# Sharing the top-k product and mask among VectorE, GpSimd and ScalarE

## The chip, the cores and the metric

The kernel runs on one core of one Trainium2 chip. The metric is the device time of one execution in microseconds, taken as the median of several runs. The engines are TensorE (PE, with its weight loads shown apart as PEld), VectorE (DVE), ScalarE (ACT), GpSimd (POOL) and SyncE (SP, which issues the transfers). Each engine works through its own instructions in the order in which the program gives them and waits where an operand of another engine is not there yet.

## The reference

Attention keeps, for every query row, only the 32 largest of its 576 scores. Its output is then routed through a mixture of eight experts, each of which takes at most 80 tokens.

```python
# attention: batch 8, heads 8, sequence 576, head dimension 64
scores = scale * np.matmul(q, k.transpose(0, 1, 3, 2))
kth = np.partition(scores, -32, axis=-1)[..., -32:-31]
scores = np.where(scores >= kth, scores, -1e9)
scores = scores - np.max(scores, axis=-1, keepdims=True)
attn = np.exp(scores)
attn = attn / (np.sum(attn, axis=-1, keepdims=True) + 1e-9)
x = np.matmul(attn, v)            # then reshaped to 4608 tokens x 512
# experts: for each e the 80 tokens with the largest gate among those that chose e
h = np.maximum(x[tok_idx] @ w1[e], 0.0)
out[tok_idx] = gate_w[tok_idx, None] * (h @ w2[e])
```

## The kernel before

The attention is cut into 288 units. A unit is 128 query rows of one head (or the last 64 rows of two heads together), so it is a tile of 128 rows by 576 scores. A pair of heads `n` has 9 units: four row blocks with two heads each (`h` is 0 and then 1), and one unit with the rests of both heads (`h` is 2). There are 32 pairs of heads. Below, the position of a unit in its nine is 0 to 8; positions 1, 3, 5 and 7 are those with `h == 1`, and position 8 is the one with `h == 2`.

A unit passes through these stages.

```python
def front(self, n, t):      # TensorE: scores of one row block; ScalarE: into SBUF, times 2^-48
    ...
    nc.scalar.activation(s[...], ps[...], Act.Copy, scale=TINY)

def parts(self, i):         # VectorE: the 8 largest of each of 6 sixths of the row -> 48 candidates
    for j in range(NG):
        nc.vector.max(out=cand[:, j, :], in_=s[:, j * S // NG : (j + 1) * S // NG])
        yield

def search(self, i):        # VectorE: the 24th largest; then ranks 25 to 32 from the row itself
    for r in range(G0 // 8):                                   # G0 = 24
        nc.vector.max(out=dst, in_=cand)
        if r == G0 // 8 - 1:
            sign = self.rows.tile([P, S], BF16, name="sign", tag="sign")
            nc.scalar.activation(sign, s, Act.Sign, bias=w9[:, 7:8], scale=-1.0, accum_out=cnt)
        yield
        if r < G0 // 8 - 1:
            nc.vector.match_replace(out=cand, in_to_replace=dst, in_values=cand, imm_value=LOW)
            yield
    y = self.rows.tile([P, S], F32, name="y", tag="y", bufs=1)        # one buffer
    nc.vector.tensor_tensor(out=y, in0=s, in1=sign, op=Alu.mult)      # the product
    yield
    nc.vector.max(out=w9[:, 8:], in_=y)                               # max of the product
    yield
    nc.vector.scalar_tensor_tensor(out=pick, in0=past, scalar=cnt, in1=w9[:, 7:],
                                   accum_out=self.thr[:, i : i + 1], ...)   # the threshold
    yield

def below(self, i):         # GpSimd: 1 where the score is below the threshold
    engine = nc.vector if i == NU - 1 else nc.gpsimd
    engine.tensor_scalar(self.mask[i], self.s[i], self.thr[:, i : i + 1], None, op0=Alu.is_lt)

def turn_w(self, n, t):     # TensorE: transposed scores, minus the transposed mask; ScalarE: Exp
    ...                     # transposes of s into PSUM (tiles ab and cc)
    nc.tensor.matmul(dst[h][c], lhsT=mk[:, keys[c]], rhs=minus, ...)  # minus = -1 on the diagonal
    nc.scalar.activation(wT[...], cc[...], Act.Exp, scale=scale / TINY)
    nc.scalar.activation(wT[...], ab[...], Act.Exp, scale=scale / TINY)
```

As the scores carry a factor of 2^-48 and the Exp takes it back, a mask of 1 becomes minus 2^48 in the exponent, and the weight becomes 0. `back` multiplies the weights by v (with a column of ones for the sums), `over` takes the reciprocal of the sums on VectorE, `divide` applies it on ScalarE, and `norm` stores the rows and forms the gates.

The stages of several units are interleaved by hand. Step `i` hands out VectorE's work by a string of letters:

```python
back = dict(a=0, b=1, c=1, d=1, e=1, y=2, g=3, h=4, m=4)
for c in "GhmbGcGdGeGGgayz":
    # G: one of the six maxima of unit i's sixths    a: the first max over its candidates
    # b, d: match_replace of unit i-1   c, e: max of unit i-1; with e goes its Sign on ScalarE
    # y: the product of unit i-2   g: the max of the product of unit i-3
    # h: the threshold of unit i-4   m: its mask   z: the reciprocals
    ...
if whole(i - 4): self.turn_w(*units[i - 4][:2])     # where h is 1 or 2
...                                                  # divide
if busy: self.front(*units[i + 4][:2])               # where h of unit i+4 is 0 or 2
if whole(i - 5): self.back(*units[i - 5][:2])
...                                                  # turn of the next q and k, norm
```

Of the kernel before, what the change touches and what calls it, by code (L numbers as in the profile page):

```python
# [10 lines left out]
BF16 = mybir.dt.bfloat16  # L11
# [3 lines left out]
Act = mybir.ActivationFunctionType  # L15
Alu = mybir.AluOpType
# [3 lines left out]
EPS = 1e-9  # L20
LOW = -3.0e38
FAR = 1e-30
TINY = 2.0 ** -48


@with_exitstack
def kernel(
# [11 lines left out]
    nc = tc.nc  # L39
# [8 lines left out]
    scale = 1.0 / math.sqrt(D)  # L48
    P = 128
# [15 lines left out]
    const = ctx.enter_context(tc.tile_pool(name="const", bufs=1))  # L65
# [5 lines left out]
    ident = const.tile([P, P], F32, name="ident")  # L71
# [26 lines left out]
    minus = const.tile([P, P], BF16, name="minus")  # L98
    nc.scalar.mul(minus, ident, -1.0)

    w1_t, w2_t = {}, {}

    def load_w(e, pool, parts=1):
# [19 lines left out]
    class Attention:  # L123


        def __init__(self, stack, lean):
            self.lean = lean
            pool = lambda name, bufs, **kw: stack.enter_context(tc.tile_pool(name=name, bufs=bufs, **kw))
            self.nat, self.qkp, self.rows = pool("nat", 1), pool("qkp", 2), pool("rows", 2)
            self.small, vpool = pool("small", 4), pool("vpool", 1)  # L130
            self.ps_s, self.ps_w, self.ps_c = (pool(n, k, space=PSUM) for n, k in (("ps_s", 1), ("ps_w", 1), ("ps_c", 2)))
            self.qk, self.turned, self.lg = {}, {}, {}
            self.s, self.top, self.cnt, self.y, self.mask, self.w, self.xn = ({} for _ in range(7))
            self.thr, self.z = thr_all, z_all


            self.vb = []
            for j in range(1 if lean else 3):
                t = vpool.tile([P, NK, 2, D + 1], F32, name=f"vb{j}")
                nc.gpsimd.memset(t[:, :, :, D : D + 1], 1.0)  # L140
                nc.gpsimd.memset(t[: P - TL, NF, :, :], 0.0)
                self.vb.append(t)

            self.xT = vpool.tile([P, NK * P], F32, name="xT")
            nc.gpsimd.memset(self.xT[:, S:], 0.0)
# [40 lines left out]
        def front(self, n, t):  # L186
# [12 lines left out]
            for h in range(g):  # L199
                self.s[i + h] = s[:, h * S : (h + 1) * S]  # L200
            nc.scalar.activation(s[:, : g * S].rearrange("p (j c) -> p j c", c=HS), ps[:, : 2 * g, :HS], Act.Copy, scale=TINY)  # L201

# [9 lines left out]
        def search(self, i):  # L212

            s, cand = self.s[i], self.top[i]
            top = self.top[i] = self.small.tile([P, G0 // 8 - 1, 8], F32, name="top", tag="top")
            w9 = self.small.tile([P, 16], F32, name="w9", tag="w9")
            for r in range(G0 // 8):
                dst = top[:, r, :] if r < G0 // 8 - 1 else w9[:, :8]
# [4 lines that stand above are left out]
                    cnt = self.small.tile([P, 1], F32, name="cnt", tag="cnt")  # L223
# [3 lines that stand above are left out]
                    nc.vector.match_replace(out=cand, in_to_replace=dst, in_values=cand, imm_value=LOW)  # L227
                    yield
            y = self.rows.tile([P, S], F32, name="y", tag="y", bufs=1)
            nc.vector.tensor_tensor(out=y, in0=s, in1=sign, op=Alu.mult)  # L230
            yield
            nc.vector.max(out=w9[:, 8:], in_=y)  # L232
            yield
            pick = self.small.tile([P, TOP_K - G0 + 1], F32, name="pick", tag="pick")
            nc.vector.scalar_tensor_tensor(out=pick, in0=past, scalar=cnt, in1=w9[:, 7:], accum_out=self.thr[:, i : i + 1],  # L235
                                           op0=Alu.is_equal, op1=Alu.mult)
            yield

        def below(self, i):

            self.top.pop(i)
            self.mask[i] = self.rows.tile([P, S], BF16, name="mask", tag="mask", bufs=3)

            engine = nc.vector if i == NU - 1 else nc.gpsimd
            engine.tensor_scalar(self.mask[i], self.s[i], self.thr[:, i : i + 1], None, op0=Alu.is_lt)  # L245
# [19 lines left out]
        def turn_w(self, n, t):  # L265

            i = n * UPP + 2 * t
            g = 2 if t < NF else 1
            ab = self.ps_w.tile([P, 2, NF, P], F32, name="ab", tag="ab")
            cc = self.ps_c.tile([P, 512], F32, name="cc", tag="cc")  # L270
            keys = [slice(c * P, c * P + P) for c in range(NF)] + [slice(S - P, S)]
            dst = [[ab[:, h, c, :] for c in range(NF)] + [cc[:, h * P : (h + 1) * P]] for h in range(g)]

            for h in range(g):
                sc = self.s.pop(i + h)
                for c in range(NK):
                    nc.tensor.matmul(dst[h][c], lhsT=sc[:, keys[c]], rhs=ident, start=c == 0 or (c == NF and h == 0), stop=False,  # L277
                                     is_transpose=True, skip_group_check=True)
            for h in range(g):
                mk = self.mask.pop(i + h)  # L280
                for c in (NF, *range(NF)):
                    nc.tensor.matmul(dst[h][c], lhsT=mk[:, keys[c]], rhs=minus, start=False, stop=True, skip_group_check=True)  # L282
            wT = self.rows.tile([P, 2 * NK, P], F32, name="wT", tag="wT")
            nc.scalar.activation(wT[:, 2 * NF : 2 * NF + g, :].rearrange("p h r -> p (h r)"), cc[:, : g * P], Act.Exp,  # L284
                                 scale=scale / TINY)
            nc.scalar.activation(wT[:, : g * NF, :], ab.rearrange("p h c r -> p (h c) r")[:, : g * NF, :], Act.Exp, scale=scale / TINY)  # L286
            self.w[n, t] = wT, cc
# [95 lines left out]
        def run(self, slow):  # L383

            units = []
            for n in range(NP):
                for t in range(NF):
                    units += [(n, t, 0), (n, t, 1)]
                units.append((n, NF, 2))
            first, second = {}, {}  # L390
            later = []
            due = []
# [7 lines left out]
            def step(i, last):  # L400
                if 0 <= i < NU:
                    n, t, h = units[i]
# [6 lines left out]
                    first[i] = self.parts(i)  # L409

                back = dict(a=0, b=1, c=1, d=1, e=1, y=2, g=3, h=4, m=4)
                for c in "GhmbGcGdGeGGgayz":
                    if c == "G":
                        if 0 <= i < NU:
                            next(first[i])
                    elif c == "a":
                        if 0 <= i < NU:
                            next(first[i], None)
                            second[i] = self.search(i)
                            next(second[i])  # L420
                    elif c == "z":
                        for u in drawn:
                            self.over(*u)
                    elif c == "m":
                        if 0 <= i - back[c] < NU:
                            self.below(i - back[c])
                    elif i - back[c] in second:
                        next(second[i - back[c]])
# [27 lines left out]
            with tc.manual_schedule():  # L456
# [4 lines left out]
                i = -4  # L461
# [233 lines left out]
    def finish(wpool, full):  # L695
# [85 lines left out]
        def judge():  # L781


            least = sl.tile([P, 4], F32, name="least")
            nc.vector.tensor_reduce(least[:, 0:1], thr_all, axis=AX, op=Alu.min)
            nc.vector.tensor_reduce(least[:, 1:2], z_all.rearrange("p n c h -> p (n c h)"), axis=AX, op=Alu.min)
            nc.vector.tensor_scalar(least[:, 1:2], least[:, 1:2], -FAR, None, op0=Alu.add)
            for i, most in enumerate((TOP - 1, cap)):
                nc.vector.tensor_scalar(least[:, 2 + i : 3 + i], count[:, i : i + 1], -1.0, most + 0.5, op0=Alu.mult, op1=Alu.add)
            one = sl.tile([P, 1], F32, name="one")  # L790
            nc.vector.tensor_reduce(one, least, axis=AX, op=Alu.min)
            ps = ps_x.tile([P, 512], F32, name="jp", tag="x")
            nc.tensor.transpose(ps[:1, :P], one, ident)
            low = sl.tile([1, 1], F32, name="low")
            nc.vector.tensor_reduce(low, ps[:1, :P], axis=AX, op=Alu.min)
            nc.vector.tensor_scalar(bad, low, 0.0, None, op0=Alu.is_le)
# [78 lines left out]
```

## Time and profile before

The time is 1110.77 us, the median of 3 runs from 1108.79 to 1112.42 us. The profiled run has a span of 1108.5 us. Attention is the part of it up to about 957 us, where the last mask starts; then come routing and the experts.

| engine | busy, us | share of the span |
|---|---|---|
| VectorE | 978.4 | 88% |
| TensorE | 936.7 | 85% |
| TensorE weight loads | 745.3 | 67% |
| ScalarE | 711.1 | 64% |
| GpSimd | 513.4 | 46% |

The shares are averages over the whole span, and they hide that the part after attention leaves VectorE, ScalarE and GpSimd nearly idle. To see what bounds attention, the span has to be read in stretches, and then the chain of work that ended last.

### The profile page before, as it was taken

The page shows a single profiled execution, that of the slowest core. Times are in us where ns is not written, and L with a number is a line of the kernel's source. Part 1 is how long each engine was busy: PE and PEld are TensorE (multiplying, and loading weights), DVE is VectorE, ACT ScalarE, POOL GpSimd, SP SyncE. Part 2 cuts the span into 40 slices and gives each one's busy share as a digit, 9 for nine tenths or more (in the row PEclk, how much of TensorE's full clock was granted, in tenths as well). Part 3 has the DMA queues.
Part 4 walks back from the last instruction along what each step waited for, and adds up shares of the span by engine and source line. Part 5 has one row for each costly group of instructions (what it writes and reads, how often), then busy time and mean ns, then how long its engine had stood idle before and what let it go on. Part 6 is the DMA issues. An engine that isn't in the chain of part 4 may idle for free.

```text
span 1108.5 us, 36039 instructions
## 1 busy us (share of the span) xinstructions
PE 936.7 (85%) x13381; PEld 745.3 (67%) x13381; DVE 978.4 (88%) x5214; ACT 711.1 (64%) x1542; POOL 513.4 (46%) x331
## 2 busy tenths in 40 slices
PE   5889888888888988888888888887988888769896
PEld 3767666666676766667666666666766666658786
DVE  4999999999999999999999999999999999771110
ACT  3777777777777777777677777776777777500110
POOL 1555555555455555555455555554455555401110
PEclk9999999999999999999999999999999999888999
DMA  4244443333333222233322211111111100043911
GB/s 97 62 120 120 112 111 79 83 83 83 83 83 72 70 67 71 73 83 82 81 72 74 82 45 44 45 44 45 44 43 43 32 18 12 13 163 119 361 53 29
DMA packets 167896, 85.79 MB, mean 77 GB/s; under 512 B 117792, under 2 KB 154656, under 8 KB 167712
## 3 DMA queue, kind: packets, MB, share of 16 engines
q1 hardware_dynamic: 166688, 80.78, 26.7%
q0 software_dynamic: 1024, 2.62, 0.8%
q8 instruction: 107, 1.75, 0.7%
q14 instruction: 77, 0.63, 0.2%
HBM read 63.19 MB, written 20.19 MB: 75 GB/s over the span
## 4 chain that ended last, share of the span: by engine, by line
DVE 84%; PE 12%; ACT 2%; another core or an unknown queue 1%; issue 0%; DMA 0%; POOL 0%; SPq 0%; POOLq 0%; DVEq 0%; ACTq 0%
DVE cand L208 25%; DVE y L230 19%; DVE w L232 17%; DVE cand L227 9%; DVE top L219 6%; DVE pick L235 3%; PE yp L765 3%; DVE w L219 3%; PE warm L621 2%; DVE z_all L312 1%; PE sp L196 1%; PE cc L300 1%; PE acc L690 0%; PE ab L277 0%
## 5 line engine op out<-in xcount | busy, mean ns | idle before, releaser
L245 POOL TENSOR_SCALAR mask<-s,thr_all 128x576 bf16<-128x576 f32 x287 | 494.0, 1721 | 465.8 <-DVE cand L227 455.9
L208 DVE MAX8 cand<-s 128x8 f32<-128x96 f32 x1728 | 399.2, 245 | 9.4 <-ACT s L201 9.4
L224 ACT ACTIVATE sign<-s,w 128x576 bf16<-128x576 f32 x288 | 225.9, 784 | 101.6 <-DVE w L219 98.3
L300 PEld LDWEIGHTS cc<-vb,wT 128*64 128x64 f32 x5760 | 213.5, 146 | 65.6 <-ACT wT L286 41.1
L300 PE MATMUL cc<-vb,wT 128*64 128x65 f32 x5760 | 236.0, 233 | 2.8 <-ACT wT L286 2.8
L196 PE MATMUL sp<-kT,qT 64*128 64x288 f32 (+1 forms) x1280 | 211.2, 451 | 14.7 <-ACT part L344 6.1
L230 DVE TENSOR_TENSOR y<-s,sign 128x576 f32<-128x576 f32 x288 | 218.5, 759 | 3.9 <-ACT sign L224 3.6
L232 DVE MAX8 w<-y 128x8 f32<-128x576 f32 x288 | 213.6, 742 | 0.0
L282 PEld LDWEIGHTS <-mask 128*128 128x128 bf16 x1440 | 92.6, 98 | 145.1 <-POOL mask L245 143.0
L277 PE MATMUL ab<-ident,s 128*128 128x128 f32 x1152 | 176.9, 282 | 1.8 <-ACT wT L286 1.7
L201 ACT ACTIVATE s<-sp 128x1152 f32<-128x1152 f32 (+1 forms) x160 | 166.9, 1043 | 16.0 <-PE sp L196 15.9
L282 PE MATMUL cc<-minus,mask 128*128 128x128 bf16 x288 | 64.8, 225 | 119.2 <-POOL mask L245 118.3
L286 ACT ACTIVATE wT<-ab 128x1024 f32<-128x1024 f32 (+1 forms) x160 | 150.5, 941 | 0.1
L196 PEld LDWEIGHTS sp<-kT,qT 64*128 64x128 f32 (+1 forms) x1280 | 109.0, 184 | 54.9 <-ACT part L344 8.0
L277 PEld LDWEIGHTS ab<-ident,s 128*128 128x128 f32 x1152 | 128.5, 142 | 25.3 <-ACT wT L286 15.9
L219 DVE MAX8 top<-cand 128x8 f32<-128x48 f32 x576 | 110.4, 192 | 0.1
L227 DVE MATCH_REPLACE8 cand<-top,cand 128x48 f32<-128x48 f32 x576 | 110.2, 191 | 0.0
L282 PE MATMUL ab<-minus,mask 128*128 128x128 bf16 x1152 | 110.1, 220 | 0.0
L321 ACT ACTIVATE xn<-cc,z_all 128x64 f32<-128x64 f32 (+1 forms) x320 | 82.8, 316 | 31.4 <-DVE z_all L312 31.4
L277 PE MATMUL cc<-ident,s 128*128 128x128 f32 x288 | 79.2, 275 | 0.1
L284 ACT ACTIVATE wT<-cc 128x256 f32<-128x256 f32 (+1 forms) x160 | 58.7, 367 | 27.2 <-PE cc L282 25.9
L235 DVE SCALAR_TENSOR_TENSOR pick<-past,cnt,w 128x9 f32<-128x9 f32 x288 | 60.8, 211 | 0.0
(186 smaller groups left out, 812.2 us busy)
## 6 DMA issues: line engine op xcount, KB each, us to landing
w<-in_moe_w_dram SPq DMA_DIRECT2D x32, 512.0 KB, 4.4
w<-in_moe_w_dram SPq DMA_DIRECT2D x8, 2048.0 KB, 13.1
out_dram<-zero SPq DMA_DIRECT2D x9, 1024.0 KB, 5.9
qn<-in_q_dram SPq DMA_DIRECT2D x64, 128.0 KB, 2.5
kn<-in_k_dram SPq DMA_DIRECT2D x64, 128.0 KB, 2.5
vb<-in_v_dram SPq DMA_DIRECT2D x64, 128.0 KB, 2.5
xd<-xn SPq DMA_DIRECT2D x32, 256.0 KB, 4.3
qn<-in_q_dram SPq DMA_DIRECT2D x32, 32.0 KB, 2.4
```

The costliest lines, as they stand in the source:

```text
L196: nc.tensor.matmul(o, lhsT=qT[d, t * P : t * P + m], rhs=kT[d, j * HS : (j + 1) * HS], start=True, stop=True)
L201: nc.scalar.activation(s[:, : g * S].rearrange("p (j c) -> p j c", c=HS), ps[:, : 2 * g, :HS], Act.Copy, scale=TINY)
L208: nc.vector.max(out=cand[:, j, :], in_=s[:, j * S // NG : (j + 1) * S // NG])
L219: nc.vector.max(out=dst, in_=cand)
L224: nc.scalar.activation(sign, s, Act.Sign, bias=w9[:, 7:8], scale=-1.0, accum_out=cnt)
L227: nc.vector.match_replace(out=cand, in_to_replace=dst, in_values=cand, imm_value=LOW)
L230: nc.vector.tensor_tensor(out=y, in0=s, in1=sign, op=Alu.mult)
L232: nc.vector.max(out=w9[:, 8:], in_=y)
L245: engine.tensor_scalar(self.mask[i], self.s[i], self.thr[:, i : i + 1], None, op0=Alu.is_lt)
L277: nc.tensor.matmul(dst[h][c], lhsT=sc[:, keys[c]], rhs=ident, start=c == 0 or (c == NF and h == 0), stop=False, is_transpose=True, skip_gr ...
L282: nc.tensor.matmul(dst[h][c], lhsT=mk[:, keys[c]], rhs=minus, start=False, stop=True, skip_group_check=True)
L300: nc.tensor.matmul(cc[r : r + TL, o], lhsT=wT[:, j * NF + c if c < NF else 2 * NF + j, r0 : r0 + TL], rhs=vb[:, c, h, :], start=(c == 0), ...
```

## The change

For the 128 units of positions 1, 3, 5 and 7 ("odd" in the code) the product `y` goes from VectorE to GpSimd, and the mask goes from GpSimd to ScalarE. There the mask is no comparison but Relu(threshold - score): positive below the threshold, 0 elsewhere. It can be as small as one rounding step of a score, so it is multiplied by a diagonal of minus 2^100 in place of minus 1. Products of all units still share one buffer `y`, so a product cannot start until the max of the product before it has been taken, and the order of the letters is changed with it: in a step whose product is GpSimd's, the product comes directly behind the max `g` that frees the buffer, and in the others it stays near the end. The purpose is to relieve VectorE by engines that have time left.

```diff
+    huge = const.tile([P, P], BF16, name="huge")
+    nc.scalar.mul(huge, ident, -HUGE)                 # HUGE = 2.0 ** 100
 ...
             y = self.rows.tile([P, S], F32, name="y", tag="y", bufs=1)
-            nc.vector.tensor_tensor(out=y, in0=s, in1=sign, op=Alu.mult)
+            engine = nc.gpsimd if i in self.odd else nc.vector
+            engine.tensor_tensor(out=y, in0=s, in1=sign, op=Alu.mult)
 ...
             self.mask[i] = self.rows.tile([P, S], BF16, name="mask", tag="mask", bufs=3)
+            if i in self.odd:
+                nc.scalar.activation(self.mask[i], self.s[i], Act.Relu, bias=self.thr[:, i : i + 1], scale=-1.0)
+                return
 ...
-                    nc.tensor.matmul(dst[h][c], lhsT=mk[:, keys[c]], rhs=minus, ...)
+                    nc.tensor.matmul(dst[h][c], lhsT=mk[:, keys[c]], rhs=huge if i + h in self.odd else minus, ...)
 ...
+            self.odd = {i for i, unit in enumerate(units) if unit[2] == 1}
 ...
-                for c in "GhmbGcGdGeGGgayz":
+                for c in "hmgyGbGcGdGGGeaz" if i - 2 in self.odd else "hmgGbGcGdGeGGyaz":
```

One more VectorE instruction on a single column, near the end, adapts a test on the smallest threshold to the new mask (`least` in the diff's last part); it runs once.

More of the change, by code (lines that the diff above doesn't have):

```diff
@@ L22 @@
 FAR = 1e-30
+HUGE = 2.0 ** 100
 TINY = 2.0 ** -48
@@ L134, in __init__ @@
             self.thr, self.z = thr_all, z_all
+            self.odd = set()
             self.vb = []
@@ L281, in turn_w @@
                 for c in (NF, *range(NF)):
-                    nc.tensor.matmul(dst[h][c], lhsT=mk[:, keys[c]], rhs=minus, start=False, stop=True, skip_group_check=True)
+                    nc.tensor.matmul(dst[h][c], lhsT=mk[:, keys[c]], rhs=huge if i + h in self.odd else minus, start=False, stop=True, skip_group_check=True)
             wT = self.rows.tile([P, 2 * NK, P], F32, name="wT", tag="wT")
@@ L785, in judge @@
             nc.vector.tensor_reduce(least[:, 0:1], thr_all, axis=AX, op=Alu.min)
+            nc.vector.tensor_scalar(least[:, 0:1], least[:, 0:1], -1.0 / HUGE, None, op0=Alu.add)
             nc.vector.tensor_reduce(least[:, 1:2], z_all.rearrange("p n c h -> p (n c h)"), axis=AX, op=Alu.min)
```

## The prediction

> **What bounds the kernel now.** I read the busy shares in 40 slices first, because totals mix attention with what comes after it:
>
> ```profile
> PE   5889888888888988888888888887988888769896
> DVE  4999999999999999999999999999999999771110
> ACT  3777777777777777777677777776777777500110
> POOL 1555555555455555555455555554455555401110
> ```
>
> VectorE is full from the second slice to about the 34th, that is, through all of attention; ScalarE is at seven tenths and GpSimd at five. Asked for the stretch of 25 to 957 us, the view by stretches gives:
>
> ```profile
> 25.00:957.00 932.00, 798.84 (x10817) 624.59 (x10813) 931.13 (x5043) 683.23 (x1477) 489.15 (x285) 0.97 0.26 68
> ```
>
> The columns are length, PE, PEld, DVE, ACT and POOL busy, granted clock, DMA share, GB/s. VectorE works 931.13 of 932.00 us. The only wait that the list of waits has for it there is 0.3 us, for a sign. So attention lasts as long as VectorE's instructions do. The chain that ended last says the same:
>
> ```profile
> DVE 84%; PE 12%; ACT 2%; another core or an unknown queue 1%; issue 0%; DMA 0%; POOL 0%; SPq 0%; POOLq 0%; DVEq 0%; ACTq 0%
> DVE cand L208 25%; DVE y L230 19%; DVE w L232 17%; DVE cand L227 9%; DVE top L219 6%; DVE pick L235 3%; PE yp L765 3%; DVE w L219 3%; PE warm L621 2%; DVE z_all L312 1%; PE sp L196 1%; PE cc L300 1%; PE acc L690 0%; PE ab L277 0%
> ```
>
> The product is 19% of it: 0.19 x 1108.5 / 288 = 0.73 us for each unit. The groups show what it and its neighbours cost:
>
> ```profile
> L245 POOL TENSOR_SCALAR mask<-s,thr_all 128x576 bf16<-128x576 f32 x287 | 494.0, 1721 | 465.8 <-DVE cand L227 455.9
> L224 ACT ACTIVATE sign<-s,w 128x576 bf16<-128x576 f32 x288 | 225.9, 784 | 101.6 <-DVE w L219 98.3
> L230 DVE TENSOR_TENSOR y<-s,sign 128x576 f32<-128x576 f32 x288 | 218.5, 759 | 3.9 <-ACT sign L224 3.6
> L232 DVE MAX8 w<-y 128x8 f32<-128x576 f32 x288 | 213.6, 742 | 0.0
> ```
>
> For the length of a step I took the timeline of VectorE and of GpSimd around 506 us:
>
> ```profile
> 505.19 0.76 DVE L230 TENSOR_TENSOR y<-s,sign 128x576 f32<-128x576 f32 x1
> 505.87 0.25 DVE L208 MAX8 cand<-s 128x8 f32<-128x96 f32 x1
> 506.04 0.21 DVE L235 SCALAR_TENSOR_TENSOR pick<-past,cnt,w 128x9 f32<-128x9 f32 x1
> 506.18 0.08 DVE L235 DVE_READ_ACCUMULATOR pick<-past,cnt,w 128x1 f32 x1
> ...
> 507.56 0.74 DVE L232 MAX8 w<-y 128x8 f32<-128x576 f32 x1
> 508.23 0.19 DVE L219 MAX8 top<-cand 128x8 f32<-128x48 f32 x1
> 508.41 0.76 DVE L230 TENSOR_TENSOR y<-s,sign 128x576 f32<-128x576 f32 x1
> ```
>
> ```profile
> 506.45 1.72 POOL L245 TENSOR_SCALAR mask<-s,thr_all 128x576 bf16<-128x576 f32 x1 [1.49 <-DVE cand L227]
> ```
>
> Durations overlap, so starts count: the product holds VectorE from 505.19 to 505.87, 0.68 us, and there are 0.18 us from the `top` to the product, where a `top` elsewhere is followed after 0.11. The rest of the step, 505.87 to 508.41, is 2.54 us. The mask starts 0.19 us after the threshold (506.18 + 0.08 to 506.45) and ends at 508.17, before the next product at 508.41.
>
> **What the Trainium skill says.** (1) "SBUF — State Buffer", section "Who interferes with whom": a VectorE instruction with two SBUF inputs contends with a GpSimd instruction that reads SBUF; one with a single SBUF input and outside the two-port modes doesn't. In the trace the 31 products between 449 and 550 us last 757 to 760 ns, and those I followed lie clear of the masks; the maxima, with one input, last 245 ns beside a mask or not. So the trace agrees on the second half and doesn't show the first. (2) "GPSIMD Engine Reference", section 3.1: a `tensor_tensor` of 2048 fp32 takes 4497 ns on GpSimd. In proportion, 576 elements are an estimate of 1.26 us; with some fixed cost and a bf16 input I take 1.35. No run here shows it, and the mask's 1721 ns for one input warns that it may be more. (3) "ScalarE: Activation LUTs", section "What ACT_TABLE_LOAD costs": with a pointer bias 280 + 0.833 N ns, and neighbours overlap by 93 ns. For 576 that is 760; the trace's Sign has 784, which I use for the Relu. Section "Table sets: the hidden batching unit" has Relu in every set; the trace agrees, with one table load in all although Sign, Exp and Relu are used.
>
> **The change part by part.**
>
> *Products leave VectorE.* 128 units x 0.73 us (0.68 for the instruction, about 0.06 for the gap ahead of it) = 93 us.
>
> *GpSimd's product in an ordinary odd step.* It may start when `g` has freed the buffer and must be done when `g` comes again. A step without its product is 2.54 + 0.09 for the reciprocal - 0.06 for the gap = 2.57 us; `g` takes 0.67 of it (507.56 to 508.23), so 1.90 lie between. From these go 0.07 (the max's 0.74 outlasts its slot), 0.19 for GpSimd to start, as with the mask, and an estimated 0.06 for VectorE to see the end: a window of 1.58 us. A product of 1.35 fits with 0.23 to spare. Cost 0.
>
> *Where mask and product fall in one step.* If unit i-2 is at position 1, unit i-4 is at position 8, whose mask is still GpSimd's and ahead of the product. The mask starts 0.41 us into the step (0.22 for the threshold, 0.19) and ends at 2.13; the product ends at 3.48, and VectorE sees it at 3.54. It wants it at 2.57 + 0.21 for the next threshold = 2.78. That is a stall of 0.76 us, once in a pair of heads: 31 x 0.76 = 24 us back.
>
> *Relu on ScalarE.* 128 x (0.784 - 0.093) = 88 us more, off VectorE's path. ScalarE goes from 683 us to 771 in a stage of some 875: 88% on average. But three steps of nine (positions 5, 7 and 0 of unit i) have nearly all of it: Relu 0.7, Sign 0.9 with its accumulator, two Exp 1.25, two `xn` 0.5, scores copy 1.1, together 4.45 us in a step of 2.57. The Sign of the next step stands behind that and ends 7.0 us after the start of the pair of steps, where GpSimd wants it at 2.57 + 3.28 + 1.1 = 7.0. So there is no reserve, and the copies `xT`, `qT` and `kT` (0.64 each) can push it later. I put down 0.2 us for two such steps in a pair of heads: 32 x 2 x 0.2 = 13 us back.
>
> *VectorE's remaining products.* In even steps the product comes some 2.4 us into the step and the mask ends at 2.13, so they should not meet: 0.
>
> *TensorE.* Instructions and shapes are the same; the Relu mask may be there 1.0 us earlier (0.78 in place of 1.72). 799 us of 875 is 91%: close, with 118 us that it now waits for masks as the reserve.
>
> *Once:* the new diagonal and the extra instruction, under 1 us together.
>
> Sum: 1110.8 - 93 + 24 + 13 = 1055 us, 5.0% less.
>
> **The rivals.** (a) *GpSimd's product becomes the wait.* If it takes 2.2 us in place of 1.35, it is 0.62 over its window in 96 ordinary steps and 1.6 late in 31: 60 + 50 = 110 us, more than the 93 gained, and the time is about 1125. For it speaks the mask, 2.99 ns an element where the page's product has 2.2; against it, the changed order gives the product its window right behind `g`, which nobody would need for a slow one. At 1.6 us the time would be near 1075. (b) *ScalarE becomes the bound.* Its load is uneven, and a late Sign delays GpSimd's product, this the max, and this VectorE. At 0.6 us in all 96 heavy pairings it would cost 58 us: about 1100. Against it: 12% are free on average, and the light steps (position 3 and 4) let it catch up. (c) *TensorE becomes the bound.* Its 91% would have to grow by a tenth, or its clock to sink; the records show 0.97 over attention. Then the stage would stop near 880 to 900 us: 1060 to 1080. (d) *All is hidden and GpSimd is quick.* With a product of 1.1 us the one collision shrinks to 0.5 us and the Sign has reserve: about 1033.
>
> **Range and chances.** Most uncertain is GpSimd's duration, then the late Signs; both act as stalls of tenths of a microsecond in some 130 places, so 10 to 40 us. Downwards there are only the 37 us of stalls that I put in, most of which stay. I take 1030 to 1092. Faster by over 2% means under 1088.6: 0.83. Within 2%: 0.11. Slower by over 2% needs a product beyond 2.2 us: 0.06.
>
> **What the profile of the changed kernel would show.** If right: 128 GpSimd products of about 1.35 us; 160 products left on VectorE at 759 ns; VectorE still busy over nine tenths in attention, with waits of its max for GpSimd's `y` of 20 to 45 us, mostly 0.7 to 0.8 us long, one in nine units; 128 Relus of 0.78 us and ScalarE near 770 us in attention; VectorE's products rarely longer than 760 ns. If GpSimd's products are over 1.6 us, the max waits in all odd units, and (a) holds. If GpSimd's product itself waits for the Sign more than some tenths of a microsecond, (b) holds. If the candidates' maxima wait for the scores' copy, or the reciprocals for TensorE, (c) holds. Longer products or thresholds on VectorE would mean that the engines contend where I assumed they don't meet. It would be wrong in whole if attention still ended near 957 us.

## The result and the profile after

| | median, us | runs, us | ratio to before, 95% interval |
|---|---|---|---|
| before | 1111.38 | 1108.79 to 1112.42 | |
| changed | 1028.34 | 1026.38 to 1029.23 | 0.9254 [0.9231, 0.9276] |

The change takes off 83 us. The prediction had 56, and the result lies 1.7 us below its range. The busy slices of the changed kernel's page:

```profile
PE   5889999999889999989899999998999998598896
DVE  3999999999999999999999999999999999551000
ACT  3888899888888898888898888898888988401110
POOL 1444555554454545554454544555454554211101
```

VectorE still fills attention. ScalarE has gone from seven tenths to eight or nine. The stretch of attention, 25 to 880 us (columns: length, PE, PEld, DVE, ACT, POOL busy, granted clock, DMA share, GB/s):

```profile
25.00:880.00 855.00, 767.11 (x10859) 610.74 (x10857) 853.36 (x4929) 760.15 (x1612) 435.80 (x287) 1.00 0.28 74
```

VectorE works 853.36 of 855.00 us, ScalarE 760.15 (89%; predicted 88%) and TensorE 767.11 (90%; predicted 91%). The groups of the operations concerned:

```profile
L254 POOL TENSOR_SCALAR mask<-s,thr_all 128x576 bf16<-128x576 f32 x159 | 273.7, 1721 | 199.6 <-PE ab L291 130.6
L236 POOL TENSOR_TENSOR y<-s,sign 128x576 f32<-128x576 f32 x128 | 164.0, 1281 | 240.3 <-ACT sign L229 104.2
L238 DVE MAX8 w<-y 128x8 f32<-128x576 f32 x288 | 217.4, 755 | 2.2 <-POOL y L236 2.0
L236 DVE TENSOR_TENSOR y<-s,sign 128x576 f32<-128x576 f32 x160 | 118.2, 739 | 3.1 <-ACT sign L229 2.6
L250 ACT ACTIVATE mask<-s,thr_all 128x576 bf16<-128x576 f32 x128 | 99.5, 777 | 0.4 <-DVE pick L241 0.4
L241 DVE SCALAR_TENSOR_TENSOR pick<-past,cnt,w 128x9 f32<-128x9 f32 x288 | 83.6, 290 | 0.0
```

GpSimd's product takes 1281 ns (I took 1350), the Relu 777 (784). Three things are not as foretold: VectorE's max shows hardly any wait for GpSimd's product, 2.0 us in place of 20 to 45; its own products are shorter, 739 ns in place of 759; and the threshold `pick`, 211 ns before, has a mean of 290. The timelines of VectorE and GpSimd at one long threshold (start, duration, instruction) show the last:

```profile
509.69 0.21 DVE L224 MAX8 top<-cand 128x8 f32<-128x48 f32 x1
509.81 1.00 DVE L241 SCALAR_TENSOR_TENSOR pick<-past,cnt,w 128x9 f32<-128x9 f32 x1
510.75 0.08 DVE L241 DVE_READ_ACCUMULATOR pick<-past,cnt,w 128x1 f32 x1
510.82 0.76 DVE L238 MAX8 w<-y 128x8 f32<-128x576 f32 x1
```

```profile
507.75 1.72 POOL L254 TENSOR_SCALAR mask<-s,thr_all 128x576 bf16<-128x576 f32 x1 [4.60 <-DVE pick L241]
509.51 1.28 POOL L236 TENSOR_TENSOR y<-s,sign 128x576 f32<-128x576 f32 x1
```

This is the foretold collision: a mask of position 8 and behind it the product of position 1. But VectorE's stall isn't shown as idle time of the max. It is inside the threshold, which starts at 509.81 and ends at 510.81, just after GpSimd's product (509.51 + 1.28 = 510.79). Taken by position, only the thresholds of position 0 are long, 907 ns on average; two others in the whole run exceed 300 ns. The page puts 130.6 us of GpSimd's idle time before its masks down to TensorE, as if a mask had waited for its buffer; but every mask of position 8 starts 0.19 us after the end of its own threshold, as in the kernel before, so the collision isn't a lack of mask buffers.

### The profile page after: what moved, and what is told of

Read it like the earlier page. It is cut to its first block, busy times and chain, and to the rows that moved or that the text cites. A ratio compares the mean times of both kernels' runs of the same rounds, so it can differ in the third digit from the quotient of the medians.

```text
span 1027.5 us, 35579 instructions
## 1 busy us (share of the span) xinstructions
PE 902.3 (88%) x13381; PEld 728.9 (71%) x13381; DVE 896.0 (87%) x5087; ACT 786.2 (77%) x1671; POOL 456.1 (44%) x331
## 4 chain that ended last, share of the span: by engine, by line
DVE 54%; PE 30%; ACT 11%; issue 2%; another core or an unknown queue 1%; DMA 0%; SPq 0%; POOL 0%; POOLq 0%; ACTq 0%; DVEq 0%
DVE cand L213 17%; DVE w L238 12%; PE cc L309 7%; DVE cand L232 6%; DVE y L236 6%; DVE pick L241 4%; DVE top L224 4%; PE yp L776 3%; PE sp L201 3%; PE ab L286 3%; ACT wT L295 3%; PE sp L178 2%; ACT sign L229 2%; PE warm L632 2%; DVE w L224 2%
## 5 line engine op out<-in xcount | busy, mean ns | idle before, releaser
L213 DVE MAX8 cand<-s 128x8 f32<-128x96 f32 x1728 | 387.0, 244 | 9.5 <-ACT s L206 9.5
L254 POOL TENSOR_SCALAR mask<-s,thr_all 128x576 bf16<-128x576 f32 x159 | 273.7, 1721 | 199.6 <-PE ab L291 130.6
L309 PEld LDWEIGHTS cc<-vb,wT 128*64 128x64 f32 x5760 | 201.2, 139 | 111.5 <-ACT wT L295 94.6
L236 POOL TENSOR_TENSOR y<-s,sign 128x576 f32<-128x576 f32 x128 | 164.0, 1281 | 240.3 <-ACT sign L229 104.2
L309 PE MATMUL cc<-vb,wT 128*64 128x65 f32 x5760 | 223.4, 225 | 52.1 <-ACT wT L295 52.1
L201 PE MATMUL sp<-kT,qT 64*128 64x288 f32 (+1 forms) x1280 | 202.0, 435 | 14.7 <-ACT part L353 6.1
L236 DVE TENSOR_TENSOR y<-s,sign 128x576 f32<-128x576 f32 x160 | 118.2, 739 | 3.1 <-ACT sign L229 2.6
L224 DVE MAX8 top<-cand 128x8 f32<-128x48 f32 x576 | 114.4, 199 | 0.1
L250 ACT ACTIVATE mask<-s,thr_all 128x576 bf16<-128x576 f32 x128 | 99.5, 777 | 0.4 <-DVE pick L241 0.4
L241 DVE SCALAR_TENSOR_TENSOR pick<-past,cnt,w 128x9 f32<-128x9 f32 x288 | 83.6, 290 | 0.0
```

Source lines behind the costliest of these rows:

```text
L201: nc.tensor.matmul(o, lhsT=qT[d, t * P : t * P + m], rhs=kT[d, j * HS : (j + 1) * HS], start=True, stop=True)
L236: engine.tensor_tensor(out=y, in0=s, in1=sign, op=Alu.mult)
L309: nc.tensor.matmul(cc[r : r + TL, o], lhsT=wT[:, j * NF + c if c < NF else 2 * NF + j, r0 : r0 + TL], rhs=vb[:, c, h, :], start=(c == 0), ...
```

## The experiments

The kernels are compared with the kernel before on the same chip; where I speak of sums, they are intervals from the start of a VectorE instruction to the start of the next, added up by kind over the trace. "Nine units" is the mean time for a pair of heads, the time from the first threshold to the last times 9/287: 29.42 us before, 26.90 changed.

**1. The order of the letters alone.** The kernel before, with VectorE keeping every product:

```diff
-                    for c in "GhmbGcGdGeGGgayz":
+                    for c in "hmgGbGcGdGeGGyaz":
```

> The kernel before with only the letters reordered, in all steps as the changed kernel has them where VectorE keeps the product; no work moves to another engine. Theory (part of the gain is the order, not the engines): the product now comes long after the max that frees its buffer, so the gap of 0.065 us goes and the products shrink from 759 to about 740 ns: 288 x (0.065 + 0.02) = 24 us less, about 1087 us, ratio 0.978. Rival (the order is only there to make the engines fit): 1111 us, ratio 1.00.

Measured: 1084.12 us, ratio 0.9765 [0.9745, 0.9786]; nine units take 28.55 us, and the products 738 ns, as the theory had it. So 26.6 us, nearly a third of what the whole change brings, are to be had without moving any work.

**2. Two buffers for the product.** The kernel before in its own order. Two product buffers beside three mask buffers don't fit: the last pool of tiles needs 10.1875 KB per partition, and 9.5625 would be left. So one mask buffer goes.

```diff
-            y = self.rows.tile([P, S], F32, name="y", tag="y", bufs=1)
+            y = self.rows.tile([P, S], F32, name="y", tag="y", bufs=2)
-            self.mask[i] = self.rows.tile([P, S], BF16, name="mask", tag="mask", bufs=3)
+            self.mask[i] = self.rows.tile([P, S], BF16, name="mask", tag="mask", bufs=2)
 ...                                   # a second tile with the tag "y" likewise
```

> The kernel before with two buffers for the product (and two for the mask in place of three, to make room), nothing else changed. In it the product starts 0.18 us after the short max ahead of it, where such a max is elsewhere followed after 0.11 us. Theory (one buffer): the product waits for the max of the product before it; with two buffers the gap goes, 288 x 0.065 = 19 us, and perhaps the 0.02 us of the product itself: 1087 to 1093 us, ratio 0.98. Rival (a product can't follow a short max any closer, whatever the buffer): 1110 us, ratio 1.00, and the gap stays at 0.18 us.

Measured: 1078.22 us against 1104.59 on that chip, ratio 0.9763 [0.9747, 0.9780]. VectorE's timeline of this kernel:

```profile
509.56 0.73 DVE L232 MAX8 w<-y 128x8 f32<-128x576 f32 x1
510.22 0.18 DVE L219 MAX8 top<-cand 128x8 f32<-128x48 f32 x1
510.33 0.73 DVE L230 TENSOR_TENSOR y<-s,sign 128x576 f32<-128x576 f32 x1
510.98 0.24 DVE L208 MAX8 cand<-s 128x8 f32<-128x96 f32 x1
```

The product starts 0.11 us after the short max, not 0.18, and holds VectorE for 0.65 us, not 0.68. Nine units take 28.53 us, the same as with the new order. So the gap was a wait of VectorE for itself, and one that the lists of waits don't show, as the recorded short max lasts until the product starts. The product had to wait for the max that still read the one buffer: before, it starts 0.11 us after the end of that max (507.56 + 0.74 = 508.30 to 508.41 in the timeline shown with the prediction), and here 0.04 us (510.29 to 510.33). A second buffer or a longer way between the two takes it away. The gain is a little more than I expected, 2.4% against some 2%.

**3. The masks alone.** The changed kernel with all products on VectorE, and the order of experiment 1:

```diff
-            engine = nc.gpsimd if i in self.odd else nc.vector
-            engine.tensor_tensor(out=y, in0=s, in1=sign, op=Alu.mult)
+            nc.vector.tensor_tensor(out=y, in0=s, in1=sign, op=Alu.mult)
-                for c in "hmgyGbGcGdGGGeaz" if i - 2 in self.odd else "hmgGbGcGdGeGGyaz":
+                for c in "hmgGbGcGdGeGGyaz":
```

> The changed kernel with all products back on VectorE and the order of the reordered kernel in all steps, so that against that kernel (1084.1 us) only the odd masks have moved, from GpSimd to ScalarE. Theory (VectorE bounds, ScalarE has room for 128 Relus where the step before is light): 1084 us within 6, ratio 0.976. Rival (a Relu stands behind the Exps and copies in ScalarE's order, as at position 8, and TensorE and the reciprocals wait): 1095 to 1110 us.

Measured: 1082.48 us, ratio 0.9750 [0.9726, 0.9775]; nine units 28.55 us. The Relus cost nothing as long as VectorE sets the pace at 28.55.

**4. The products alone.** The changed kernel with every mask left on GpSimd (the set that decides on the Relu, and on the 2^100 diagonal, is left empty):

```diff
-            if i in self.odd:
+            if i in self.soft:            # empty
                 nc.scalar.activation(self.mask[i], self.s[i], Act.Relu, ...)
```

> The changed kernel with all masks on GpSimd (none is a Relu), products as in the changed kernel. Theory (mask and product in one step on GpSimd overrun the window): each odd step has the mask until 2.13 us and then the product of 1.28, done at 3.41 to 3.5 where VectorE asks at 2.78: 127 stalls of about 0.7 us in place of 31, so 1028 + 96 x 0.7 = 1095 us, ratio 0.986, and the long thresholds are at positions 0, 2, 4 and 6. Rival (ScalarE without the Relus is freer, and this pays for it): 1060 us or less.

Measured: 1097.32 us, ratio 0.9878 [0.9854, 0.9903], 2 us from the theory, and slower than the new order with no work moved (1084.12). GpSimd's timeline:

```profile
399.44 1.72 POOL L254 TENSOR_SCALAR mask<-s,thr_all 128x576 bf16<-128x576 f32 x1 [1.46 <-DVE pick L241]
401.13 1.28 POOL L236 TENSOR_TENSOR y<-s,sign 128x576 f32<-128x576 f32 x1
402.64 1.72 POOL L254 TENSOR_SCALAR mask<-s,thr_all 128x576 bf16<-128x576 f32 x1 [0.23 <-DVE pick L241]
```

Now every odd step has mask and product in a row, and the thresholds of positions 0, 2, 4 and 6 last 910, 798, 795 and 840 ns; what thresholds take beyond 211 ns adds up to 80.7 us, against 23.6 us in the changed kernel. So the Relu is what makes the move pay: it is there to empty GpSimd ahead of the product.

**5. Who holds the threshold.** The changed kernel, the max ahead of the threshold in the even steps:

```diff
-  "hmgGbGcGdGeGGyaz"
+  "ghmGbGcGdGeGGyaz"
```

> The changed kernel with the max g ahead of the threshold h in the even steps; no work is moved. The threshold of position 0 lasts 907 ns in the changed kernel though it reads nothing that GpSimd's product writes. Theory (it has two SBUF inputs and can't run beside GpSimd's product; the max behind it would have had to wait for the product anyway): the time stays at 1028 us within 5, no threshold is longer than 250 ns, and the max is shown to wait for GpSimd's product, some 20 us in all. Rival (the threshold waits for operands of its own): it stays at 0.9 us.

Measured: 1034.72 us, ratio 0.9326 [0.9305, 0.9347]. The threshold's instructions and the waits of VectorE in this kernel (minimum, median and maximum in ns; total us and times):

```profile
L241 DVE SCALAR_TENSOR_TENSOR pick<-past,cnt,w x288: 200/211/230, 25.9 to 885.9; 128x9 f32<-128x9 f32 x144
...
DVE w L238 <- POOL y L236: 29.3, 35, 2.2
```

No threshold is longer than 230 ns, and the wait has become visible at the max, which needs the product. The threshold reads nothing that GpSimd writes; it was held only while GpSimd's product ran. The Trainium skill, "SBUF — State Buffer", section "Who interferes with whom", says just this of a VectorE instruction with two SBUF inputs beside a GpSimd instruction that reads SBUF, and here the trace agrees: held until the product's end, 0.70 us beyond its 0.21. It cost nothing of its own, since the max behind it would have waited too. Against what I expected the time is 6 us longer than the changed kernel's, where I had allowed 5; the wait at the max (29.3 us) is longer than the excess of the thresholds with their accumulator reads had been (28.6 us by the sums), which explains little of it. The two profiled executions differ by 2.3 us only (spans of 1029.8 and 1027.5). The rest I leave open.

**6. The collision taken away by ScalarE.** The changed kernel, position 8 with a Relu as well:

```diff
-            if i in self.odd:
+            if i in self.soft:            # positions 1, 3, 5, 7 and 8
```

> The changed kernel, with the mask of position 8 as Relu on ScalarE too, so that no step has a mask and a product on GpSimd. In the changed kernel the threshold of position 0 lasts 907 ns on average where the others last 211. Theory (GpSimd's product, pushed back by that mask, holds up VectorE): the 907 fall to about 211 and the time by 31 x 0.70 = 22 us: 1006 us, ratio 0.905 to before. Rival (ScalarE is the bound or close to it): it gets 32 x 0.69 = 22 us more work, late Signs take the gain back, and the time stays at 1020 to 1035 us.

Measured: 1091.29 us, ratio 0.9834 [0.9806, 0.9863], 63 us slower than the changed kernel and far outside both theories: the gain is not just taken back. ScalarE isn't full, 745.20 of 875 us from 25 to 900. Its timeline, and then TensorE's:

```profile
483.03 1.03 ACT L295 ACTIVATE wT<-ab 128x1024 f32<-128x1024 f32 x1
483.93 0.54 ACT L330 ACTIVATE xn<-cc,z_all 128x64 f32<-128x64 f32 x2
484.32 1.16 ACT L206 ACTIVATE s<-sp 128x1152 f32<-128x1152 f32 x1
485.33 0.81 ACT L250 ACTIVATE mask<-s,thr_all 128x576 bf16<-128x576 f32 x1
```

```profile
484.61 0.27 PE L286 MATMUL cc<-ident,s 128*128 128x128 f32 x1
486.20 0.23 PE L291 MATMUL cc<-huge,mask 128*128 128x128 bf16 x1 [1.33 <-ACT mask L250]
```

The Relu of position 8 stands behind the Exps, the scalings and the scores' copy of the step before, and TensorE stops for it 1.33 us. From 25 to 900 us, TensorE's waits for a Relu at this matmul (total us, times, longest) are, here and then in the changed kernel:

```profile
PE cc L291 <- ACT mask L250: 52.6, 60, 1.3
PE cc L291 <- ACT mask L250: 12.7, 30, 0.4
```

In the changed kernel GpSimd has that mask ready at the same place, and TensorE goes straight on, at 455.15 and 455.26:

```profile
455.15 0.27 PE L286 MATMUL cc<-ident,s 128*128 128x128 f32 x1
455.26 0.22 PE L291 MATMUL cc<-minus,mask 128*128 128x128 bf16 x1
```

What TensorE loses there comes back at VectorE, which waits with its reciprocals for TensorE (17.0 us, 34 times), with the gates for ScalarE (14.1 us) and with products for Signs (9.7 us). So the Relus came late from an engine that had 15% to spare. That its order alone made the loss isn't shown; experiment 12 tries it.

**7. Position 8 treated like the odd ones**, product and mask:

```diff
-            self.odd = {i for i, unit in enumerate(units) if unit[2] == 1}
+            self.odd = {i for i, unit in enumerate(units) if unit[2] > 0}
```

> The changed kernel, with position 8 treated like the odd positions: its mask is a Relu and its product is GpSimd's, 160 products in all. Theory (VectorE is the bound as long as the product fits its window of 1.58 us): 22 us as in the run with the Relu alone, and 32 x 0.68 = 22 us for the products: 984 us, ratio 0.886. Rival (ScalarE, then 97% busy by sums, or TensorE at 95%, becomes the bound): 995 to 1010 us, with VectorE waiting for Signs or scores, no better than the Relu alone.

Measured: 1085.74 us, ratio 0.9757 [0.9722, 0.9791] (one of the four executions, 1098.56 us, fell in a slower state with a lower granted clock, and the ratio leaves it out). Neither expectation holds. Another 32 products off VectorE change the ratio of experiment 6, 0.9834, by less than one per cent: by then VectorE no longer sets the pace.

**8 to 10. The collision taken away without ScalarE.** Three ways, all from the changed kernel. The first takes threshold and mask of position 8 a step earlier, the second leaves the product of position 1 to VectorE, the third gives VectorE the mask of position 8 (in short):

```diff
+  # 8: H and M are the threshold and the mask of unit i-3
+  "hmgGyHMbGcGdGGGeaz" where i % 9 == 2, then "gyGbGcGdGGGeaz" where i % 9 == 3
+  # 9: masks as in the changed kernel; the step of position 1 gets the letters of the even steps
+  self.odd = {i for i in self.soft if i % UPP > 1}
+  # 10
+  engine = nc.vector if i % UPP == UPP - 1 else nc.gpsimd
```

> The changed kernel with the threshold and the mask of position 8 taken one step earlier, behind the product on VectorE, so that GpSimd has that mask done before the product of position 1; no work is moved to another engine. Theory (the stall behind that mask is VectorE's own loss, of which the late Sign of position 1 leaves a part): between 31 x 0.47 = 15 and 22 us less, 1006 to 1013 us, ratio about 0.909. Rival (the stall hides waits of the loop through ScalarE and TensorE, which come out at the reciprocals once it is gone): 1022 to 1030 us.

> The changed kernel with the product of position 1, the one that stands behind a mask on GpSimd, left on VectorE; its mask stays a Relu, and the other three odd products stay on GpSimd. In the changed kernel that product costs VectorE a stall of 0.70 to 0.83 us where its own would cost 0.66. Theory (moving this product gained nothing): 31 x (0.83 - 0.66) = 5 us less, about 1020 to 1026 us, and no threshold over 0.3 us at position 0. Rival (the product did pay, since VectorE would have waited there for ScalarE and TensorE anyway): 1035 us or more, with new waits of the reciprocals or products.

> The changed kernel with the mask of position 8 on VectorE, where the one such mask of the kernel before lasted 520 ns. Theory (the stall is taken away at the price of the mask, and ScalarE gets nothing more to do): 31 x (0.83 - 0.45) = 12 us less, about 1016 us, ratio 0.914. Rival (the loop through ScalarE and TensorE needs about 26.8 us for nine units whatever VectorE does, as in the kernel with the early mask): 1022 to 1030 us, with waits at other places.

| | time, us | ratio, 95% interval | nine units, us | threshold at position 0 and 4, ns |
|---|---|---|---|---|
| changed | 1028.34 | 0.9254 [0.9231, 0.9276] | 26.90 | 907, 227 |
| 8: early mask | 1024.88 | 0.9240 [0.9211, 0.9269] | 26.77 | 262, 510 |
| 9: three products | 1027.10 | 0.9255 [0.9242, 0.9267] | 26.78 | 212, 277 |
| 10: mask on VectorE | 1027.38 | 0.9255 [0.9243, 0.9268] | 26.84 | 214, 365 |

The threshold's durations in 8, 9 and 10 (minimum, median and maximum in ns; the changed kernel has 1003), and the only wait of VectorE that the list of 8 has from 25 to 860 us:

```profile
L241 DVE SCALAR_TENSOR_TENSOR pick<-past,cnt,w x288: 168/213/614, 23.0 to 876.5; 128x9 f32<-128x9 f32 x144
L241 DVE SCALAR_TENSOR_TENSOR pick<-past,cnt,w x288: 168/211/383, 25.0 to 879.0; 128x9 f32<-128x9 f32 x144
L241 DVE SCALAR_TENSOR_TENSOR pick<-past,cnt,w x288: 168/212/612, 22.9 to 878.9; 128x9 f32<-128x9 f32 x144
...
DVE w L238 <- POOL y L236: 2.0, 1, 2.0
```

The stall at position 0 goes in all three, and the time hardly moves. In 8 and 10 part of it comes back at once: the thresholds of position 4 are held, as GpSimd's product of position 5 starts late behind its Sign. In 9 there is little left to hold, but VectorE has a product more: by the sums, thresholds with their accumulator reads take 23.9 us less and VectorE's products 20.4 us more. Its theory said this, with a time about 1 us lower: moving the product of position 1 gains nothing. In 10 the thresholds with their reads take 15.2 us less and the mask 13.5 us more. For 8 and 10 the times of the rivals came true, but not their reason: no wait of the reciprocals shows, and in 9 and 10 VectorE's thresholds, products and mask account for the time, so that three equal ends don't prove a limit set by ScalarE or TensorE. No version is clearly ahead of the changed kernel.

**11 and 12. The scores three steps ahead.** Experiments 8 and 6 with ScalarE's copy of the scores moved from the step with the Relu and the Exps to the next:

```diff
-                busy = 0 <= i + 4 < NU and units[i + 4][2] != 1
+                busy = 0 <= i + 3 < NU and units[i + 3][2] != 1
-                    self.front(*units[i + 4][:2])
+                    self.front(*units[i + 3][:2])
```

> The kernel with the early mask of position 8 (1024.9 us), with the scores of a pair of units made three steps ahead instead of four, so that ScalarE's copy of the scores falls into the step after that with the Relu and the Exps. There the thresholds of position 4 lasted 510 ns, as GpSimd's product waited for a Sign that stood behind that copy. Theory (it is the order on ScalarE, not its load, that brings the Sign late): no threshold over 0.3 us, and the step sums fall from 26.8 to some 26.2 us for nine units: 32 x 0.6 = 19 us less, about 1006 us, ratio 0.907. Rival (ScalarE and TensorE, both 90% busy, are the bound): 1020 us or more, the wait comes out elsewhere.

> The kernel with the Relu of position 8 on ScalarE (1091.3 us), with the scores made three steps ahead instead of four. There that Relu stood behind the Exps, the scalings and the copy of the scores and came 1.3 us after TensorE asked for it. Theory (the order on ScalarE made the loss, since ScalarE was 85% busy only): without the copy ahead of it, 1.1 us, the Relu comes in time and most of the loss goes: 1005 to 1045 us. Rival (the 32 Relus are more than ScalarE can take): 1080 us or more.

Measured: 1075.04 us, ratio 0.9734 [0.9718, 0.9751], and 1086.06 us, ratio 0.9833 [0.9816, 0.9849]. Both theories were wrong. The times lie in the ranges of the rivals, but their reason isn't shown: in the first, ScalarE is busy 738.58 and TensorE 724.04 of the 875 us from 25 to 900. The waits of VectorE in the first, up to 860 us:

```profile
DVE z_all L321 <- PE cc L309: 25.9, 38, 1.8
DVE y L236 <- ACT sign L229: 24.9, 29, 0.9
DVE lg L356 <- ACT part L353: 8.9, 21, 0.4
```

The thresholds are no longer held (none over 0.37 us), but the reciprocals wait for TensorE, and products for Signs. The edit moved more than I meant: the turning of the next q and k and the stages of `norm` take the steps without scores, so they moved too, in front of the products with v. The two runs therefore don't tell whether another order on ScalarE could do better; they show only that VectorE's instructions aren't what sets the time there.

## Why the prediction was wrong

By its own steps, rounded, measured between the first and the last threshold (24.8 to 963.1 us before, 23.2 to 880.9 changed: 80.5 us less; the last threshold and its mask, on VectorE, come behind the 957 us given above as the end of attention):

| step | predicted, us | measured, us | from |
|---|---|---|---|
| 128 products leave VectorE | -93 | -95 | 128 x (0.676 + 0.065), product and gap |
| collision at position 1 | +24 | +27 | thresholds of position 0 with their accumulator reads |
| late Signs | +13 | +2 | the two other long thresholds and remainders |
| VectorE's remaining products | 0 | -13 | 160 x (0.065 + 0.019) |
| rest of attention | 0 | -1 | remainder |
| ahead of the first and behind the last threshold | 0 | -0.5 | -1.7 and +1.2 |
| medians of the times against the profiled executions | | -2 | 83.0 - 80.5 - 0.5 |

**What was right.** VectorE bounded, and its product was worth 0.73 to 0.74 us. GpSimd's product fits its window; the page's 4497 ns for 2048 elements ("GPSIMD Engine Reference", section 3.1) gave 1.26 us, and the trace has 1.281. The collision was placed and sized well, 0.70 us longer thresholds for 0.76, though it sat in the threshold and not in a wait of the max. ScalarE's and TensorE's loads came out within 2%.

**What failed: "VectorE's remaining products ... 0".** I saw the gap of 0.06 us ahead of the product, counted it as a gain where the product leaves, and did not ask why it was there. Experiments 1 and 2 show the cause: the single buffer made the product wait for the max of the product before. The new order separates them also in the 160 units whose product stays. I had the new order before me and read it only as what gives GpSimd its window. That term is -13 us in place of 0.

**What failed: the late Signs.** I put in 13 us for Signs that delay GpSimd's product, and 2 came. The Signs were late: GpSimd waited 104.2 us for them, 21.0 of it ahead of its first product. But at position 1 the Sign isn't what holds the product: it ended 0.69 us (median) before the product starts, and the mask ends last. At position 5 the product starts 0.17 us after its Sign, 0.45 us after the max that frees the buffer, where a product that no Sign holds back starts after 0.15. That is 0.30 us late, more than the 0.2 that I charged, and yet the threshold beside it, of position 4, lasts 227 ns on average: I had worked out 0.23 us to spare in the window and set nothing of it against the 0.2, and the product is 0.07 us shorter than I took it. The collision also takes lateness away: the Sign of position 5 ends 0.16 us after the freeing max on average, but 0.57 and 0.40 us after it in experiments 8 and 10, without the collision, and there the thresholds of position 4 are held. That the 0.7 us in nine units let ScalarE catch up is my reading of these figures. The two stalls stand in for one another, and I added them. These two terms, 13 and 11 us, are nearly all of the 27 us between 1055 and 1028.

**The rivals.** (a) fell with 1.281 us. The working for 1.6 us gives about 1064 us, not 1075: 0.02 in 96 steps and 1.01 in 31 are 33 us, with the 13 us of late Signs. (b) and (c) did not set the time, yet they are nearer than I gave them: in experiments 6, 11 and 12, VectorE waits for both. How much the changed kernel itself could gain before they bind isn't settled. The chain that ended last of the changed kernel hints that it is little:

```profile
DVE 54%; PE 30%; ACT 11%; issue 2%; another core or an unknown queue 1%; DMA 0%; SPq 0%; POOL 0%; POOLq 0%; ACTq 0%; DVEq 0%
```

VectorE had 84% of that chain before; now PE and ACT have 41% of it, although VectorE is busy 853 of 855 us.

## What to carry to other kernels

A small regular gap ahead of an instruction on the busiest engine deserves its cause before anything else: here one buffer that was read until just before it was written cost 26 us, and a second buffer or another order of the letters gave it back without moving any work. When work is moved to engines with time to spare, ask at which place of their own order it lands and who waits there in order; the share of free time doesn't tell that. Stalls that feed on the same slack are not added, since removing one can let the other appear; and a delay is set against the time to spare before it is charged.

## What the runs showed of the hardware

A wait can hide inside a busy instruction: a threshold of 128x9 elements lasted up to 1003 ns beside GpSimd's product, and the profile counts that as VectorE at work, with 0.0 us idle ahead of it. TensorE's granted clock was 1.00 in attention of the changed kernel against 0.97 before, although it was busier (90% against 86%); no run was made to find out why.
